# Loading v of two batch pairs through the SP queue in transfers of eight partitions

## The chip, the cores and the metric

The kernel runs on one core of one Trainium2 chip. The metric is the device time of one execution in microseconds (us). A profiled execution has a span some 1.7 us shorter than its time, and all readings "at 400.66 us" count from the start of the span.

## The reference

Attention with a decay over 8 batches and 8 heads (576 positions, head dimension 64), then a mixing of 64 Fourier modes by complex 512 x 512 weights, then a channel mix. Cut to what matters:

```python
scores = scale * q @ k.T + cumulated_log_decay      # causal, softmax, times v
x = attention.transpose(0, 2, 1, 3).reshape(8, 576, 512)
X = rfft(x, axis=1)[:, :64]
Y = einsum('bmd,mde->bme', X, w_r + 1j * w_i)        # 2 x 64 x 512 x 512 floats
u = x + irfft(Y)
out = u + relu(u @ w_ch)
```

The mode weights are read once, 134 MB in float32. They make the kernel bound by DMA.

## The kernel before

The program walks through 16 batch pairs of attention and, between their steps, multiplies the mode weights as they arrive. Nearly every load is issued by GpSimd in one fixed order; the transfers of weights, k and q also convert float32 to bfloat16 on the way. The v of a pair stays float32. It goes into one of three staging buffers (`STG = 3`); the first pair's v already comes by the SP queue.

```python
def pool_dma(dst, src):
    keep(nc.gpsimd.dma_start(dst, src))          # one order for all GpSimd loads
# ... cut ...
def emit_loads(pr):
    dc, bp, _ = steps[2 * pr]
    for nm, src in (("k", k), ("q", q), ("v", v)):
        one = src[2 * bp, 2 * dc, :, :]
        dst = QKVst[pr % STG][nm][:, :, :, :].rearrange("p b r d -> p b (r d)")
        ap = bass.AP(tensor=one.tensor, offset=one.offset,
                     ap=[[NR * Dh, 128], [H * S * Dh, 2], [1, NR * Dh]])
        if nm == "v" and pr < 1:
            nc.sync.dma_start(dst, ap)
        else:
            pool_dma(dst, ap)
# ... cut: in emit_transposes, the only reader of v ...
ins = nc.vector.tensor_tensor(sb, st, wdec9_of_this_pair, ALU.mult)
```

`NR * Dh` is 9 x 64 = 576 floats. So v of a pair is 128 partitions x 2 batches x 2,304 bytes, in all 576 KB.

The softmax here doesn't subtract the row's maximum and nothing guards it: scores larger than these inputs give would overflow.

## Time and profile before

| | before |
|---|---|
| time, median of 3 runs | 437.25 us (436.92 to 439.48) |
| profiled span | 437.0 us (that execution took 438.78 us) |
| last weight transfer has landed on all 16 DMA engines | 400.66 us |
| from there to the end | 36.3 us |
| landings of that transfer, first to last engine | 392.63 to 400.66 us |
| v of the 9th pair: issued, read | 88.11, 122.82 us |

The profile has a strip for DMA (one digit for each fortieth of the span, 9 is busy for 90% or more), a table of queues (packets, MB, the time of their packets as a share of sixteen engines' span), and a chain of waits (start, length, what). The trace has two finer records: a semaphore increment for each engine that finishes its share of a transfer, and the start and length of each DMA packet. Neither names an engine. The increments of a transfer therefore tell how far apart the engines are. "Offset" below is an engine's increment minus that of the foremost engine for the same transfer.

### The profile page before, as it was taken

Reading aid. Unit: us, or ns where it says so; the run is one execution under the profiler, and the core shown is the slowest. Engines: PE = TensorE matmul, PEld = TensorE weight load, DVE = VectorE, ACT = ScalarE, POOL = GpSimd, SP = SyncE. Lnnn points to the kernel's source line nnn. Section 1 sums busy time; section 2 is a strip of 40 time slices with the busy share of each in tenths; the row PEclk is TensorE's granted clock in tenths of the full one; section 3 lists DMA queues with packets and bytes.
Section 4 is the critical chain, followed back from the end, with each engine's and each line's share of the span. In section 5 each row is a group of like instructions: output and inputs, shape, how many; then the busy total and the mean of one; then the engine's idle time right before and its main releaser. Section 6 shows DMA issues by size and latency. Waiting matters only on the chain.

```text
span 437.0 us, 12197 instructions
## 1 busy us (share of the span) xinstructions
PE 359.5 (82%) x5247; PEld 245.5 (56%) x5265; DVE 263.3 (60%) x658; ACT 224.6 (51%) x340; POOL 128.9 (29%) x202
## 2 busy tenths in 40 slices
PE   3787799998897887978778796999999688998880
PEld 2454666676666665656556664666665354554440
DVE  5797778877565655655657677333334353753891
ACT  2887478775534537446355473234335242742780
POOL 7333332233233233232332231323232223200600
PEclk9996699998866858556668688699999898998997
DMA  8999999999999999999999999999999999993797
GB/s 185 233 235 244 230 236 238 237 214 234 233 215 236 228 220 237 211 237 233 215 237 211 211 212 211 211 211 211 211 211 212 211 211 211 211 207 73 253 366 270
DMA packets 50981, 97.37 MB, mean 223 GB/s; under 512 B 3792, under 2 KB 12976, under 8 KB 50928
## 3 DMA queue, kind: packets, MB, share of 16 engines
q0 software_dynamic: 46688, 86.16, 100.6%
q1 hardware_dynamic: 3920, 9.91, 6.3%
q8 instruction: 41, 0.67, 0.6%
q10 hardware_dynamic: 320, 0.52, 0.5%
q14 instruction: 12, 0.10, 0.1%
HBM read 163.73 MB, written 9.44 MB: 396 GB/s over the span
## 4 chain that ended last, share of the span: by engine, by line
PE 31%; DMA 29%; ACT 12%; DVE 11%; issue 4%; ACTq 0%; DVEq 0%; POOL 0%
DMA wb<-in_moe_w_i_dram 27%; ACT E L574 8%; PE pav L612 7%; PE ps L567 6%; PE A L188 5%; PE tp L305 5%; DMA stv<-in_v_dram 3%; DVE QTs L320 2%; PE px L655 2%; PE vp L539 2%; ACT KT L318 2%; PE pz L826 2%; PE pu L826 1%; DVE os L1004 1%; DVE XT L669 1%
## 5 line engine op out<-in xcount | busy, mean ns | idle before, releaser
L574 ACT ACTIVATE E<-ps 128x1024 bf16<-128x1024 f32 (+1 forms) x128 | 101.5, 853 | 22.8 <-PE ps L567 12.7
L188 PE MATMUL A<-XT,wb 128*128 128x16 bf16 x1984 | 70.3, 181 | 14.6 <-DMA wb<-in_moe_w_i_dram 9.6
L188 PEld LDWEIGHTS <-wb 128*128 128x128 bf16 x1984 | 63.5, 99 | 28.6 <-issue 11.9
L93 POOL DMA_DIRECT2D wb<-in_moe_w_r_dram x64 | 42.5, 664 | 120.7 <-DMA wb<-in_moe_w_r_dram 24.5
L567 PE MATMUL ps<-QTs,KT 64*128 64x64 bf16 (+4 forms) x384 | 57.6, 320 | 18.2 <-ACT E L574 16.3
L93 POOL DMA_DIRECT2D wb<-in_moe_w_i_dram x64 | 42.4, 663 | 86.6 <-DMA wb<-in_moe_w_i_dram 42.9
L612 PE MATMUL pav<-va,E 128*128 128x65 bf16 (+1 forms) x1088 | 55.5, 210 | 3.1 <-DVE x_all L634 2.6
L612 PEld LDWEIGHTS <-E 128*128 128x128 bf16 (+1 forms) x1088 | 45.5, 115 | 17.5 <-issue 8.1
L589 DVE TENSOR_TENSOR E<-E,trimask 128x256 bf16<-128x256 bf16 (+2 forms) x128 | 36.9, 303 | 20.2 <-ACT E L574 20.0
L324 ACT COPY VT<-tp 128x640 bf16<-128x640 bf16 (+1 forms) x32 | 23.2, 762 | 33.5 <-PE tp L305 33.5
L865 ACT CAST XW<-pxw 128x512 bf16<-128x512 f32 x36 | 20.7, 586 | 35.8 <-PE pxw L858 23.5
L567 PEld LDWEIGHTS <-KT 64*128 64x128 bf16 x384 | 19.2, 99 | 32.8 <-issue 21.1
L908 ACT CAST XW<-pB 128x512 bf16<-128x512 f32 x36 | 20.9, 586 | 31.4 <-PE pB L826 25.8
L318 ACT COPY KT<-tp 128x640 bf16<-128x640 bf16 (+1 forms) x32 | 22.0, 751 | 26.2 <-PE tp L305 26.0
L907 DVE CAST x_all<-pA 128x512 bf16<-128x512 f32 x36 | 24.9, 692 | 16.7 <-PE pA L826 15.2
L858 PE MATMUL pxw<-wch,yy 128*128 128x512 bf16 x133 | 33.7, 386 | 1.2 <-issue 0.7
L320 DVE COPY QTs<-tp 128x640 bf16<-128x640 bf16 (+1 forms) x32 | 23.3, 767 | 14.2 <-PE tp L305 14.0
L634 DVE TENSOR_TENSOR x_all<-pav,rcp 128x384 bf16<-128x384 f32 x64 | 29.2, 456 | 0.9
L153 DVE TENSOR_TENSOR YTe<-A,Yacc 128x128 bf16<-128x128 f32 x16 | 5.9, 368 | 33.2 <-PE A L188 33.2
L623 DVE RECIPROCAL rcp<-pav 128x6 f32<-128x6 f32 x64 | 12.1, 190 | 22.6 <-PE pav L612 21.8
L826 PEld LDWEIGHTS <-ident_bf 64*64 64x64 bf16 (+1 forms) x300 | 14.5, 110 | 17.0 <-issue 9.6
L539 PE MATMUL vp<-ident_bf,VT 128*128 128x128 bf16 x160 | 17.2, 249 | 4.8 <-DVE QTs L320 4.3
(143 smaller groups left out, 609.8 us busy)
## 6 DMA issues: line engine op xcount, KB each, us to landing
wb<-in_moe_w_r_dram POOLq DMA_DIRECT2D x62, 512.0 KB, 17.2
wb<-in_moe_w_i_dram POOLq DMA_DIRECT2D x62, 512.0 KB, 17.8
stv<-in_v_dram POOLq DMA_DIRECT2D x10, 576.0 KB, 15.4
out_dram<-os SPq DMA_DIRECT2D x10, 512.0 KB, 6.3
stk<-in_k_dram POOLq DMA_DIRECT2D x11, 288.0 KB, 15.4
stq<-in_q_dram POOLq DMA_DIRECT2D x11, 288.0 KB, 15.2
wx<-in_v_dram POOLq DMA_DIRECT2D x5, 576.0 KB, 15.1
out_dram<-uo SPq DMA_DIRECT2D x3, 512.0 KB, 3.6
```

Of the source, the lines that this page charges most:

```text
L93: keep(nc.gpsimd.dma_start(dst, src))
L188: nc.tensor.matmul(A[:, eb, mi, :], lhsT=w_of(mi, eb * 128), rhs=x_of(m), start=(i == 0), stop=(i == len(terms) - 1),)
L318: nc.scalar.copy(rows(KTs[pr % 2][:, :, 0:S]), tv)
L320: ins = nc.vector.tensor_copy(rows(QT[pr][:, :, :]), tv)
L539: nc.tensor.transpose(vp[:, sc, :, :].rearrange("p b d -> p (b d)"), VTs[s // 2 % 2][:, h, sc * 128 : (sc + 1) * 128], ident_bf[:, :],)
L567: nc.tensor.matmul(ps[:, b, o : o + n], lhsT=KTs[pr % 2][bs, h, jb * 128 : (jb + 1) * 128], rhs=QT[pr][bs, h, jb * 128 + c0 : jb * 128 + c ...
L574: nc.scalar.activation(E[:, :, piece * 512 : piece * 512 + w], ps[:, :, 0:w], ACT.Exp, scale=scale,)
L589: nc.vector.tensor_tensor(dg, dg, tr, ALU.mult)
L612: nc.tensor.matmul(pav[64 * half : 64 * half + w, slot, :], lhsT=E[:, b, c : c + (w - 1) * st + 1 : st], rhs=va[:, jb, b, :], start=(n == ...
L634: nc.vector.tensor_tensor(xo, pi, ri, ALU.mult)
L826: return nc.tensor.matmul(p, lhsT=lhsT, rhs=rhs, start=first, stop=not first, skip_group_check=True)
L858: nc.tensor.matmul(pxw[:, :], lhsT=xT[:, eb, i * 128 : (i + 1) * 128], rhs=wch[:, eb, :], start=(eb == 0), stop=(eb == NDC - 1),)
```

## The change

It takes v of the ninth and thirteenth pair off the GpSimd queue. Sixteen SP transfers of eight partitions take its place, presumably meant to run on eight of the sixteen DMA engines only, so that the other eight are relieved.

```diff
+    EIGHTS = (8, 12,)
...
                 if nm == "v" and pr < 1:
                     nc.sync.dma_start(dst, ap)
+                elif nm == "v" and pr in EIGHTS:
+                    for p in range(0, 128, 8):
+                        nc.sync.dma_start(
+                            dst[p : p + 8, :, :],
+                            bass.AP(
+                                tensor=one.tensor,
+                                offset=one.offset + p * NR * Dh,
+                                ap=[[NR * Dh, 8], [H * S * Dh, 2], [1, NR * Dh]],
+                            ),
+                        )
                 else:
                     pool_dma(dst, ap)
```

## The prediction

> **What bounds the kernel now.** I read the page first: the DMA strip, the queue table and the chain of work that ended last. The DMA engines are busy at 0.9 or more from the second slice until the weights have landed, the GpSimd (software) queue alone fills 100.6% of sixteen engines' span, and the largest piece of the chain is the landing of weights:
>
> ```profile
> DMA  8999999999999999999999999999999999993797
> q0 software_dynamic: 46688, 86.16, 100.6%
> q1 hardware_dynamic: 3920, 9.91, 6.3%
> q8 instruction: 41, 0.67, 0.6%
> ```
>
> Then the chain in order of time for 270 to 396 us. From 276 us on it is one weight load after another, and TensorE starts the tile before last 0.05 us after the last of them:
>
> ```profile
> 276.12 18.28 DMA wb<-in_moe_w_i_dram
> 294.40 0.29 issue
> 294.69 19.60 DMA wb<-in_moe_w_i_dram
> ...
> 375.30 19.72 DMA wb<-in_moe_w_i_dram
> 395.02 0.05 issue
> 395.07 0.91 PE A L188 x30
> ```
>
> So anything on DMA that delays the last weight delays the end one to one, and anything that only makes one stage of attention quicker is worth nothing. The tail behind the last landing (400.66 us, below) is 36.3 us of TensorE, VectorE and output and is not touched.
>
> The wait list says how GpSimd meets this: it waits for the transfer issued eight earlier, over and over. Eight software transfers are in flight, and a transfer counts as landed only when its slowest engine has finished.
>
> ```profile
> POOL wb L93 <- DMA wb<-in_moe_w_r_dram: 55.2, 31, 2.5
> POOL wb L93 <- DMA wb<-in_moe_w_i_dram: 55.2, 33, 2.7
> ```
>
> **The sixteen engines are not equally late.** The trace records each of the sixteen completion increments of every transfer. I grouped them by semaphore, sixteen to a transfer, and looked at the spread from first to last. It is 1.1 us for the first weight transfer, 2.5 us near 60 us, 3.6 us near 140, 5.1 us near 220, 6.2 us near 290 and 8.03 us at the very last weight transfer, whose increments fall from 392.63 to 400.66 us. The foremost engine is never idle: it takes 2.47 us for each weight transfer all the way through. At the last transfer the offsets from the foremost engine are 0, 0.01, 0.13, 0.19, 0.52, 0.73, 1.69, 3.29, and then 4.82, 4.93, 6.50, 6.80, 6.85, 6.97, 7.14, 8.03: eight early engines and eight late ones. The late ones move back in single steps of 1.1 to 1.5 us, and the steps fall at the times of the 41 packets of the instruction queue (16,384 bytes, median 959 ns each; their lengths repeat with a period of eight, 974, 974, 961, 893, 893, 949, 945, 936 ns). So TensorE's instruction blocks are fetched by eight engines in turn, and those eight end the weights 3 to 8 us after the others. The early engine at 3.29 moved in smaller steps, of about 0.5 us, beside the 8,192-byte instruction packets of the other engines. I take this change to be aimed at that imbalance.
>
> **What the Trainium skill says.** In "DMA: Bandwidth & Descriptors", the section on why a DMA increments its semaphore by 16 says that a DMA runs on the largest k up to 16 that divides the slowest dimension of both sides, and that from SP these are the lowest-numbered k engines. Eight partitions then mean engines 0 to 7, one partition each. The trace before has no transfer that shows it. The same page, "Queues, rings and completion order", says that an engine takes its queue rows in turn, packet by packet; the SP load of the first pair's v, 4.3 us from issue to landing against a median of 15.4 us for the GpSimd ones, agrees, though little was queued then. "Runtime: NRT & Kernel Launch", "Instruction fetch mechanics", gives 16 KiB instruction blocks; 0.67 MB in 41 packets is 16.3 KB each, which agrees. No page that I found says which engines fetch TensorE's instructions, and the trace has no engine numbers. That is the open point.
>
> **The change part by part.** Removed: two of the GpSimd transfers of v, 576 KB each. An engine's share is 8 packets of 4,608 bytes at 178 ns, 1.42 us; the completion records give 1.47 us from q's landing to v's on one engine. All sixteen engines lose 2 x 1.47 = 2.94 us. GpSimd also loses two issues of 0.73 us, which fill none of its waits.
>
> Added: 32 SP transfers of 8 x 2 x 576 floats (36 KB each). If they run on the eight lowest engines, each engine moves 16 x 2 = 32 packets of 2,304 bytes per pair. At the 93 ns that such packets took for the first pair this is 2.98 us, with 16 completion writes of 22 ns 3.33 us; at the rate of the present weights (4,096 bytes read per packet, 16 packets in 2.47 us, 26.5 bytes per ns) it would be 2.78 us. So those eight gain 5.6 to 6.7 us for the two pairs and lose 2.94: 2.6 to 3.7 us net each.
>
> Moved: the two v transfers now wait on SP for the staging buffer only (multiplies of v at 75.34 and 142.07 us), not in GpSimd's order (issues at 88.11 and 158.44). They land earlier, and their users come late anyway: the multiplies of those pairs start at 122.82 and 195.66 us, while v has landed at about 101.8 and 174.7. The emitted order confirms it: SP gains twice sixteen loads, GpSimd loses two, and TensorE and VectorE only shift a few instructions.
>
> Sum, if engines 0 to 7 are the early ones: the late eight end at 8.03 - 2.94 = 5.1, the early ones at most at 3.29 + 2.6 to 3.7 = 5.9 to 7.0. The last landing moves from 8.03 to 5.9 to 7.0, a gain of 1.0 to 2.1 us: 437.25 becomes 435.2 to 436.2. The eight early engines, not the late ones, then bound the end; that is why the whole 2.9 us can't be had.
>
> **Rivals.** (a) Engines 0 to 7 are the fetching, late ones, or the fetching ones are spread over both halves. Then the latest engine gains 2.6 to 3.7 us of work and the end moves to 439.9 to 440.9 us. Nothing in the trace rules it out. Against it speaks the shape of the change: sixteen small transfers instead of one are an odd price to pay unless the other eight engines needed relief, and two pairs take 2.9 us off an imbalance whose group means differ by about 5.7 us, about half of it, which is what levelling wants. I give the favourable case 75%.
>
> (b) The wait for v on the chain goes away. The chain has
>
> ```profile
> 88.11 11.64 DMA stv<-in_v_dram
> 99.75 0.01 issue
> 99.77 0.42 DVE Yacc L197
> 100.19 1.26 DVE vb L291
> ```
>
> which looks like 11.64 us to win, some 2.7%. But the timeline names the operand of that multiply:
>
> ```profile
> 100.10 1.35 DVE L291 TENSOR_TENSOR vb<-wx,wdec 128x1152 bf16<-128x1152 f32 x1
> ```
>
> It reads wx, another pair's v, which landed at 85.09 us; the transfer issued at 88.11 is read at 122.82, 21 us after it lands. The chain put the wait down to the semaphore's latest update. Were (b) true the time would be near 426; I give it 1%.
>
> (c) The SP issues become a wait: each transfer from the ninth on waits for the one eight before it. Sixteen issues at 0.56 us and two rounds of landings take perhaps 10 to 15 us, against 46 and 52 us from free buffer to use. It is hidden: no effect. Nor does SP have other work before 389 us.
>
> (d) Many small descriptors slow the weights on the same engines by more than their own length. This would push the early engines past 8 us and give 437.5 to 439.
>
> **Range and chances.** Weighted: 75% for 435.2 to 436.2 with some leak towards 437.5, the rest near 440.5. The weight of the favourable case puts my figure at 435.9; 434.6 to 440.6 holds both outcomes. Two per cent is 8.7 us, more than any of the sums, so within 2% is nearly certain. A slow run of the kernel before was at 439.48, so single runs will not settle this.
>
> **What would show it.** Right: in the changed kernel the last weight lands 1 to 2 us earlier than 400.66; the spread of its completion increments shrinks to 6 or 7 us; the two SP loads each put a step of 1.3 to 1.9 us on eight early engines, while the late ones draw nearer; 256 packets of v per pair on the hardware queue. Wrong: the spread grows to 10 or 11 us, with the steps on the engines that were late already (rival a); a foremost engine that idles; waits of VectorE for v; or a last landing that moves while the end does not, because the tail is bound by TensorE.

## More of the kernel before

Repeated executions of one kernel mostly agree within 0.3%, though on one of the chips used here the kernel before ranged from 436.5 to 440.7 us. Differences of under one per cent are therefore read from when work ends in the trace as well as from the times.

## The result, and the profile after

| | before, same chip | after |
|---|---|---|
| time, median | 437.7 us (436.92 to 439.48, 4 runs) | 443.22 us (441.71 to 444.41, 4 runs) |
| profiled span | 437.0 us | 441.1 us |
| last weight landed | 400.66 us | 405.46 us |
| from there to the end | 36.3 us | 35.6 us |
| landings of the last weight, first to last | 392.63 to 400.66 us | 393.06 to 405.46 us |

The ratio is 1.0119, with a 95% interval from 1.0073 to 1.0164. The change made the kernel slower by 1.2%. The prediction was 435.9 us, a gain, and its range ended at 440.6.

The page of the changed kernel, DMA strip, rate for each fortieth of the span (11.0 us), and queue table:

```profile
DMA  8999999999999999999999999999999999993697
GB/s 182 233 235 246 228 235 238 230 210 211 225 222 237 229 227 210 210 235 225 224 233 215 211 212 211 211 211 211 212 211 212 210 211 211 211 199 64 232 366 283
q0 software_dynamic: 46400, 84.98, 99.4%
q1 hardware_dynamic: 4688, 11.10, 7.3%
q8 instruction: 41, 0.67, 0.6%
```

The strip is as full as before: busy time does not show the damage, since a slow packet counts as busy. (The rate of the eighth slice, 77 to 88 us, 230 GB/s while the first v was loaded, is compared further down with that of a kernel with the same bytes in the same place.) In the table 288 packets left q0 and 768 came to q1 for the same 1.2 MB. q1's share rose from 6.3% of 437.0 us to 7.3% of 441.1 us: times sixteen engines, from about 440 us to 515 us of engine time. That is 75 us (the rounding of the shares leaves some 7 us of doubt), or 9.4 us for each of eight engines, where the prediction had put 5.6 to 6.7.

The end of the chain of waits of the changed kernel (start, length, what):

```profile
369.75 19.60 DMA wb<-in_moe_w_i_dram
389.35 0.28 issue
389.63 15.82 DMA wb<-in_moe_w_i_dram
405.46 0.05 issue
405.50 0.36 PE A L173 x8
```

Weight load follows weight load as before, and the last is 4.8 us later. One thing is different. In the chain of the kernel before, which the prediction shows to 395.07 us, the last wait for DMA ends at 395.02; from there on TensorE and VectorE are at work, and the last weight, landed at 400.66 us, is used only at 401.25, some 0.5 us later:

```profile
400.40 0.29 PE A L172 x8
400.69 0.33 PE pu L826 x2
...
401.25 0.29 PE A L172 x8
```

In the changed kernel TensorE waits for the last weight and starts 0.05 us after it. This slack is most of why the span grew by 0.7 us less than the landing moved.

No wait of VectorE for v came up. The last packets of the two SP loads start at 92.5 and 161.7 us, and the multiplies that read them at 122.83 and 195.68 us. The list of instructions that touch v (count, duration min/median/max in ns, first and last start in us):

```profile
L277 SPq DMA_DIRECT2D stv<-in_v_dram x32: 272/273/544, 76.4 to 155.7; - x32
L302 DVE TENSOR_TENSOR vb<-stv,wdec x11: 1348/1352/1359, 15.3 to 254.4; 128x1152 bf16<-128x1152 f32 x11
```

The packet records tell where the extra engine time lies. These are the 256 packets of 2,304 bytes and 128 completion writes of each SP load (tabulated from the trace of the changed kernel):

```
                 data packet mean / median     completion mean
9th pair             150.5 / 134 ns                72.9 ns
13th pair            117.6 / 106 ns                20.1 ns
```

The prediction had assumed 93 and 22 ns. The v packets of GpSimd's queue that ran beside them (4,608 bytes) had medians of 254 to 266 ns, against 178 in the kernel before.

The offsets of the last weight transfer were 0, 0.37, 3.86, 3.95, 4.05, 4.07, 4.40, 4.74, and then 6.91, 7.00, 7.25, 7.70, 8.25, 10.44, 11.39, 12.40. I followed each offset through the transfers. The latest eight are the engines that carried the SP loads; they land 7.35 us later than the same engines before, on the mean (with the identification of the eight given under "map" below). The other eight end at 397.8 us, which is the old latest landing less the 2.9 us that had been predicted as their relief. Not all of them kept it: the two foremost engines landed at 393.06 and 393.43 us, no earlier than the foremost ones before (392.63). Two of the eight SP engines (11.39 and 12.40) still take steps of about 1.1 us from instruction fetches after 200 us.

### The profile page after: what moved, and what is told of

Same layout as the page of the kernel before. It is cut to its first block, busy times and chain, and to the rows that moved or that the text cites. A ratio compares the mean times of both kernels' runs of the same rounds, so it can differ in the third digit from the quotient of the medians.

```text
span 441.1 us, 12253 instructions
## 1 busy us (share of the span) xinstructions
PE 365.1 (83%) x5247; PEld 247.6 (56%) x5265; DVE 263.5 (60%) x658; ACT 225.9 (51%) x340; POOL 127.9 (29%) x200
## 4 chain that ended last, share of the span: by engine, by line
DMA 39%; PE 29%; ACT 9%; DVE 7%; issue 4%; DVEq 0%; ACTq 0%; POOL 0%
DMA wb<-in_moe_w_i_dram 39%; PE pav L623 6%; ACT E L585 6%; PE ps L578 6%; PE A L189 5%; PE tp L316 4%; PE pz L837 2%; DVE QTs L331 2%; PE vp L550 2%; PE pu L837 2%; PE px L666 1%; ACT VT L335 1%; ACT KT L329 1%; DVE vb L302 1%; PE px L691 1%
## 5 line engine op out<-in xcount | busy, mean ns | idle before, releaser
L578 PE MATMUL ps<-QTs,KT 64*128 64x64 bf16 (+4 forms) x384 | 59.3, 326 | 16.0 <-ACT E L585 13.8
L623 PE MATMUL pav<-va,E 128*128 128x65 bf16 (+1 forms) x1088 | 58.3, 215 | 3.6 <-DVE x_all L645 3.2
L623 PEld LDWEIGHTS <-E 128*128 128x128 bf16 (+1 forms) x1088 | 47.6, 118 | 17.5 <-issue 6.0
```

The lines of the kernel that those rows point to most:

```text
L578: nc.tensor.matmul(ps[:, b, o : o + n], lhsT=KTs[pr % 2][bs, h, jb * 128 : (jb + 1) * 128], rhs=QT[pr][bs, h, jb * 128 + c0 : jb * 128 + c ...
L623: nc.tensor.matmul(pav[64 * half : 64 * half + w, slot, :], lhsT=E[:, b, c : c + (w - 1) * st + 1 : st], rhs=va[:, jb, b, :], start=(n == ...
```

## The experiments

Unless said otherwise results are correct. The kernel before had a median of 437.17 to 437.19 us beside the first eight kernels and 437.47 beside the last four.

The explanations, by the numbers that some expectations use: **1**, each transfer costs each of its engines a fixed time; **2**, the confinement to eight engines slows these; **3**, each packet of the hardware queue costs some 0.16 us beside software packets; **4**, where in SBUF the eight partitions lie slows the packets (shared write ports); **5**, the DRAM side does (the eight engines read neighbouring rows). Besides these there is the question of membership: are the eight engines of the SP loads the early ones?

| kernel | each v load | packets, 9th / 13th pair, mean ns | last weight landed, us | ratio to before (95%) |
|---|---|---|---|---|
| before, two traces | one GpSimd transfer | - | 400.66, 400.29 | 1 |
| changed kernel | 16 x 8 neighbours | 150.5 / 117.6 | 405.46 | 1.0119 (1.0073 to 1.0164) |
| one16 | one SP transfer of 128 | 104 to 105.5 | 400.21 | 1.0013 (0.9998 to 1.0028) |
| p16 | 8 x 16 neighbours | 138 / 161 | 403.00 | 1.0069 (1.0049 to 1.0089) |
| b1 | 32 x 8 neighbours, one batch each | 106.9 / 106.4 | 402.51 | 1.0066 (1.0049 to 1.0083) |
| ports | 16 x 8, every fourth partition | 104.8 / 104.0 | 402.63 | 1.0085 (1.0056 to 1.0113) |
| rowsonly | neighbours in SBUF, rows four apart | 132.5 / 111.6 | 404.16 | single look |
| portsonly | every fourth in SBUF, neighbouring rows | 103.4 / 103.6 | 402.45 | single look |
| step2 | 16 x 8, every second partition | 106.4 / 104.5 | 402.71 | single look |
| ports1 | as ports, 9th pair only | - | 400.95 | 1.0046 (1.0023 to 1.0069) |
| nov | both v loads left out | - | 397.27 | 0.9947 (0.9913 to 0.9982) |
| low4 | 9th pair, half on four engines | 106.8 | 399.53 | 0.9979 (0.9948 to 1.001) |

**one16.** Both v loads go to SP, each as one transfer of 128 partitions.

```diff
+                elif nm == "v" and pr in EIGHTS:
+                    nc.sync.dma_start(dst, ap)
```

> The two v loads on the SP queue as one transfer of 128 partitions each, so on all sixteen engines: the queue changes, the confinement to eight engines and the small transfers do not come along. In the changed kernel the eight SP engines gained about 10.3 us of work gross for the two pairs, 5.15 per pair, or 0.161 us per packet of 2,304 bytes. Theory 1 (each small transfer costs its engines about 0.13 us beyond its packets): 16 packets of 0.093 and one completion, 1.6 us per pair against 1.47 before, so the end within 0.5 us of the kernel before. Theory 2 (eight engines are slowed because the load is confined to them): no confinement, so within 0.5 us. Theory 3 (a packet of the hardware queue itself costs 0.16 us beside software packets): 2.6 us per pair against 1.47, so all engines and the end come 2.2 us later.

437.68 us, 1.0013 of before, and the last weight at 400.21 us. The SP queue by itself, over all sixteen engines, costs nothing that can be seen. Explanation 3, which wanted 2.2 us more here, falls. So the loss comes from how the load is cut up and where it runs.

**p16.** Eight transfers of sixteen neighbouring partitions, which use all engines (cut: the access pattern has 16 rows too).

```diff
-                    for p in range(0, 128, 8):
-                            dst[p : p + 8, :, :],
+                    for p in range(0, 128, 16):
+                            dst[p : p + 16, :, :],
```

> Eight SP transfers of sixteen partitions per pair: each transfer still gives an engine two packets and one completion, as in the changed kernel, but all sixteen engines share them. Theory 1 (per transfer) and theory 3 (per packet): 8 x 0.32 = 2.6 us per engine and pair against 1.47, so all sixteen engines are later by 1.1 us per pair and the end by 2.2 us against before. Theory 2 (confinement): about as before, within 0.5 us.

440.12 us, and the last weight at 403.00. Even spread over all sixteen engines, the load is dear, so the confinement (2) is not needed for it: data packets of 138 and 161 ns and completions of 31 and 50 ns give 16 x 150 + 8 x 40 ns = 2.7 us per engine and pair. The foremost engine's own landing, 395.29 against 392.63, gives 2.8 per pair when the 1.47 that it saved is added back. With the 106 ns that other cuts show it would be 1.9 us. The page of p16 and the page of one16 show the difference in engine time at nearly the same bytes, first p16:

```profile
q1 hardware_dynamic: 4688, 11.10, 7.5%
```

and one16:

```profile
q1 hardware_dynamic: 4464, 11.09, 7.1%
```

**b1.** Twice as many transfers, with one packet for each engine in each.

```diff
                     for p in range(0, 128, 8):
+                        for b in range(2):
-                            dst[p : p + 8, :, :],
+                            dst[p : p + 8, b, :],
```

> Thirty-two SP transfers of eight partitions and one batch per pair: on the same eight engines the same packets and bytes as in the changed kernel, but twice the transfers and completions. Theory 1 (0.13 us per transfer): 16 more transfers are 2 us more per pair on those engines, so the last landing some 4 us later than in the changed kernel, near 447 us. Theories 2 and 3 (confinement, or per packet): the same as the changed kernel, 442 to 444 us.

440.04 us, last weight at 402.51: 32 transfers per pair were cheaper than 16. Explanation 1 falls; the 442 to 444 us of 2 and 3 did not come either. Data packets were back at 106.9 and 106.4 ns on the same neighbouring partitions. The gross cost per SP engine and pair works out as 32 x 106.7 + 32 x 21 ns = 4.1 us. So neighbouring partitions alone don't make packets slow; it also matters how they follow one another.

**map.** A diagnostic. The v of four pairs is cut so that SP transfers have 2, 4, 8 and 12 partitions, the rest of each v by GpSimd or the same queue, so that the sets of engines nest.

```diff
+    PLAN = {
+        5: ((2, 16, "sp"), (96, 1, "pool")),
+        8: ((4, 16, "sp"), (64, 1, "pool")),
+        11: ((8, 16, "sp"),),
+        14: ((12, 10, "sp"), (8, 1, "sp")),
+    }
```

> A look, not a candidate: v of pair 5 partly on two engines (16 transfers of 2 partitions), of pair 8 partly on four (16 of 4), of pair 11 wholly on eight (16 of 8), of pair 14 on twelve (10 of 12). If a transfer of n partitions runs on the n lowest-numbered engines, the completion records fall into nested groups of 2, 2, 4, 4 and 4 engines that are later by steps, and the steps of TensorE's instruction fetches later on show to which groups the fetching engines belong. My first reading (the eight fetching engines are the upper eight) wants no such step in the first eight; the trace of the changed kernel suggests that two of the first eight fetch and two of the upper eight do not. Time several us above the changed kernel, since two engines get some 15 us more.

Last weight at 406.20 us, time 444.38 us (one look). It told three things. First, with two partitions the record can be read packet by packet: a hardware-queue packet of 106 ns, then one software packet, and so on in turn, with a completion write of 22 ns. Two data packets and a completion take 0.234 us of an engine, sixteen such transfers 3.75 us. "Queues, rings and completion order" of the skill's "DMA: Bandwidth & Descriptors" has an engine take its rows in turn by packet; the trace agrees. Second, the data packets averaged 108 ns with two partitions, 106.5 with four, 129 with eight, 190 with twelve. Third, the nesting sorts the engines by how much each was pushed back. Among the most delayed, the offsets 10.01, 11.22 and 11.95 show no late fetch steps, while 9.97 and 10.09 do. This fits engines 0 to 3 without fetches, two fetching engines among 4 to 7, two among 8 to 11 and four among 12 to 15. So the eight engines of a transfer of eight partitions are six early ones and two fetching ones. That set is consistent with the changed kernel, where exactly two of the latest eight keep fetching; low4 tests it below.

The lengths of the instruction fetches, which repeat with a period of eight, say which two they are. Only two of the eight take 893 ns. In the kernel before, the engines that end at offsets 4.82 and 4.93 make their last steps (3.43 to 4.50 and 3.35 to 4.43) beside the fetches of 893 ns at 314.8 and 323.9 us. In the changed kernel the two loaded engines step (10.78 to 11.88 and 10.32 to 11.41) beside the fetches of 893 ns at 319.1 and 328.4 us. So the fetching engines under the SP loads are the ones that stood at 4.82 and 4.93.

**ports.** Eight partitions four apart in each transfer; both sides of the copy keep their meaning.

```diff
-                    for p in range(0, 128, 8):
-                            dst[p : p + 8, :, :],
+                    for n in range(16):
+                        p = 32 * (n // 4) + n % 4
+                            dst[p : p + 29 : 4, :, :],
-                                ap=[[NR * Dh, 8], ...
+                                ap=[[4 * NR * Dh, 8], ...
```

> The changed kernel, but each transfer takes every fourth partition (p, p+4, ... p+28) instead of eight neighbours; result correct. In the record of two engines alone (16 transfers of 2 partitions) a software packet stands between every two hardware ones and a transfer costs an engine 2 x 0.106 + 0.022 = 0.234 us, 3.75 us per pair, not the 5.15 that the changed kernel shows; there the hardware packets grow to 118 to 150 ns on average, software packets of v from 178 to 254 and more. Theory 4 (eight neighbouring partitions are two SBUF ports by the port map of the Trainium skill, four engines on each; every fourth partition is eight ports): packets back at 106 ns, 3.75 us per pair, net 2.28; the latest fetching engine of the first eight, 4.93 us before, ends at about 9.5 to 10 us, so the last weight 1.5 to 2 us after that of the kernel before, the time near 439. Theory 1 (a cost per transfer as such): 443 as the changed kernel.

Packets of 104.8 and 104.0 ns and completions of 19 ns: the slow packets are gone, and the GpSimd packets of v beside them are back at about 180 ns. The last weight landed at 402.63 us, 2.0 to 2.3 us after before, and 2.8 us earlier than in the changed kernel. The remaining loss is the two fetching engines among the eight (offsets 11.91 and 11.32): they land 5.1 and 4.6 us later than the two fetching engines of the set did before.

The skill's "SBUF — State Buffer", "Door 1: The DMA port swizzle", says that four neighbouring partitions share one of sixteen DMA ports, and that the next four lie on another. Then eight neighbours reach two ports, and eight partitions four apart reach eight. That is what suggested this run, and the runs agree with it as far as the next ones show.

**rowsonly and portsonly.** Ports changed both sides of the copy at once. These two, with wrong results, change one side each: rowsonly reads DRAM rows four apart into neighbouring partitions (the destination of the changed kernel), portsonly reads neighbouring rows into every fourth partition.

```diff
 rowsonly:  dst[8 * n : 8 * n + 8, :, :]   rows p, p+4, ... p+28
 portsonly: dst[p : p + 29 : 4, :, :]      rows 8n, 8n+1, ... 8n+7
```

> Wrong result on purpose: as ports on the DRAM side (rows 4 apart), but into eight neighbouring partitions as in the changed kernel. Theory 4 (SBUF ports): slow packets and a last weight near 405 us as in the changed kernel. Theory 5 (engines that read neighbouring DRAM rows hinder each other): packets of 106 ns and a last weight near 402.5.

> Wrong result on purpose: neighbouring DRAM rows as in the changed kernel, but into every fourth partition. Theory 4 (SBUF ports): packets of 106 ns, last weight near 402.5. Theory 5 (DRAM rows): slow packets, last weight near 405.

The packets stayed slow in rowsonly (132.5 and 111.6 ns, last weight 404.16) and were fast in portsonly (103.4 and 103.6 ns, last weight 402.45). So it is the placement in SBUF, not the rows in DRAM: 5 falls, and of explanation 4 the placement is shown, the shared ports are not (see step2). Rowsonly's packets were a little shorter than the changed kernel's, but the same cut had 129 ns in map, so this lies within its own spread. The page of portsonly, to be held against that of the changed kernel at equal packets and bytes, shows it without packet records:

```profile
GB/s 179 234 235 240 235 235 238 250 220 211 233 215 236 234 237 210 210 237 230 218 236 213 211 212 211 211 211 211 211 211 211 211 211 211 211 202 78 230 364 298
...
q1 hardware_dynamic: 4688, 11.10, 7.0%
```

The eighth number is 250 instead of 230. 7.0% of 437.5 us times sixteen is 490 us, 25 us less than in the changed kernel, or 1.6 us for each of eight engines and pair.

**step2.** Eight partitions two apart, two engines to a port by the skill's map.

```diff
+                        p = 16 * (n // 2) + n % 2
+                            dst[p : p + 15 : 2, :, :],
```

> Correct, both pairs: sixteen transfers of eight partitions two apart, so that two instead of four of the eight engines write through one port of SBUF. Theory of shared ports: packets of 2,304 bytes take between those of the changed kernel (150.5 and 117.6 ns on average) and those of every fourth partition (104.8 and 104.0), nearer the latter, near 106 ns, and the last weight lands 402.5 to 403.5. If only transfers with neighbouring partitions in a run are slow, also 104 to 106. If it is something else in the pattern of the changed kernel that any eight partitions close together bring, 118 to 150 and a last landing near 405.

Packets of 106.4 and 104.5 ns, last weight 402.71 us: held, two engines on a port are not slow. But sharing of ports as such isn't the whole story. In map, four engines on one port were at 106.5 ns, and in b1 the eight neighbours were fast with one packet each. In these runs the slowing came only with transfers of eight to sixteen neighbouring partitions that put two packets on each engine. What exactly collides stays open.

**ports1.** As ports, for the ninth pair only, on the idea that half the load would leave the SP engines below the others.

> Every fourth partition, and only the ninth pair. Eight engines gain 3.75 - 1.47 = 2.28 us, the others lose 1.47. From the offsets of the kernel before: the latest fetching engine of the first eight 4.93 + 2.28 = 7.2, of the others 8.03 - 1.47 = 6.6, so the last weight 0.8 us earlier than before and the time 0.8 us less, if the loads' cost is what theory 4 says. At the changed kernel's 3.7 us net it would be 8.6, 0.6 us later than before.

438.66 us, ratio 1.0046: a loss where a gain had been expected. The two fetching SP engines came last (offsets 9.65 and 9.06). They landed 2.9 and 3.4 us later than before, where 3.75 - 1.47 = 2.3 had been worked out; so 0.6 to 1.1 us of it is not accounted for. Even at 2.3 us, the later of the two would have landed at 397.56 + 2.3 = 399.8 us, only 0.8 earlier than the end before. A load on this set of eight lands on two engines that have only some 3 us of room (8.03 less 4.93).

**before2, nov, low4** ran together on another chip.

> The kernel before, unchanged, profiled on another chip run, so that the readings by step and engine do not rest on one trace alone. Every theory: last weight landing 400.7 us to within 0.5, increments 8.0 us apart to within 0.3, two lanes near 4.8 to 5.0 between the eight early and the six late ones, the instruction fetch packets of 893 to 974 ns in a rotation of eight.

The kernel before again: 400.29 us instead of 400.66, spread 7.43 instead of 8.03 us, same two lanes at 4.97 and 5.02. The spread missed its expectation by 0.3 us, so a difference of half a microsecond in one trace's last landing means nothing here. In this trace the last weight is on the chain: TensorE starts 0.05 us after it, at 400.34 us. It also gave a warning on the chain. This is its summary for before2, where the page before has DMA at 29%, with the same program:

```profile
DMA 39%; PE 27%; ACT 10%; DVE 7%; issue 4%; DVEq 0%; ACTq 0%; POOL 0%
```

and this the one of the changed kernel:

```profile
DMA 39%; PE 29%; ACT 9%; DVE 7%; issue 4%; DVEq 0%; ACTq 0%; POOL 0%
```

The share of DMA in the chain depends on where the walk back changes from DMA to an engine that ended nearly as late. That it is higher after the change says nothing on the change.

> Wrong result on purpose: the v loads of the ninth and thirteenth pair are left out altogether, on every queue. This measures what the removed half of the change is worth by itself. The account by engine says that all sixteen engines lose 2 x 1.47 = 2.94 us, so the last weight lands 2.9 us earlier than in the kernel before (near 397.7) and the kernel takes 434.3 us; the spread of the last transfer's increments stays at 8.0 us. The rival, that the two loads filled gaps or that the end is bound elsewhere, gives less than 1.5 us. With this as the base, the added half in the changed kernel is the last landing of the changed kernel minus this one.

```diff
+                elif nm == "v" and pr in EIGHTS:
+                    pass
```

Without the two loads (wrong result) the last weight landed at 397.27 us, 3.0 to 3.4 earlier, and the time was 435.68 us, ratio 0.9947. In landing the removed half of the change is worth the predicted 2.9 us; in time it was 1.8 us by the medians (0.8 to 3.8 by the interval), less than the 2.9 us expected here too. The added half moves the landing by 405.46 - 397.27 = 8.2 us. The spread did not stay at 8 but shrank to 5.4 us: the foremost engine landed only 0.7 us earlier, and so did not use its room (at 284.9 us its next landing came 4.39 us after the one before, where 2.47 is the rule). That part of the expectation missed; the latest engine sets the last landing.

> Correct, ninth pair only. Half of v (64 partitions) by sixteen SP transfers of four partitions four apart, which the account puts on engines 0 to 3 alone, the engines that fetch no instructions; the other half by one GpSimd transfer of 64 partitions over all sixteen. Engines 0 to 3 take 16 x 4 half-size packets more: gross 3.75, less the 0.73 of the half that left the GpSimd queue and less 0.73 more of... net 3.75 - 0.73 = 3.0 us, from at most 3.3 (perhaps 4.9 for one) to at most 6.3 (7.9) behind the foremost; the other twelve lose 0.73 us. So the last weight lands 0.7 us earlier than in the kernel before and the kernel takes 436.5 us (ratio 0.998). If one of engines 0 to 3 is a fetching one after all, the last weight lands 2 to 3 us later (ratio 1.005 to 1.007). If a transfer costs the same whatever its placement, the same as the first.

```diff
+    EIGHTS = (8,)
+                    for n in range(16):
+                        p = 16 * (n // 4) + n % 4
+                        nc.sync.dma_start(dst[p : p + 13 : 4, :, :], ...)   # 4 partitions
+                    pool_dma(dst[64:128, :, :], ...)                        # the other half
```

Correct, and the only cut that gained: last weight at 399.53 us, 0.8 to 1.1 earlier than before. Four offsets took steps of about 2 to 3 us while the load ran, and the largest offset was 7.13. The time, 437.01 us with a ratio of 0.9979 (0.9948 to 1.001), is where it was expected but can't be told from none. Had one of the four engines been among the six latest, the end would have moved back by 1.5 to 3 us. This supports engines 0 to 3 as the ones without fetches. The packets, four to four ports, were at 106.8 ns.

## Why the prediction was wrong

**What held.** DMA bounds the kernel, and a later last weight means a later end: +4.8 us in landing, +4.1 us in the profiled span, +5.5 us in the medians. "One to one" is too strong: in the kernel before, the last landing had some 0.5 us of slack, and from it to the end the fourteen traces have 34.9 to 37.0 us. The relief was 2.9 us for the latest engine without the load in the changed kernel and 3.0 to 3.4 in nov. The SP loads run on eight engines: the sixteen increments of each come as one immediate update and eight landings, as the skill's section quoted in the prediction has it. The first SP transfer was issued at 76.41 us and all of v of the ninth pair had landed by about 93, so rival (c), a wait on SP, stayed hidden. Rival (b), a wait for v that goes away, did not come.

**First failing step, the size.** "each engine moves 16 x 2 = 32 packets of 2,304 bytes per pair. At the 93 ns ... with 16 completion writes of 22 ns 3.33 us". It measured (7.35 + 2.94) / 2 = 5.15 us. The terms: 32 packets at 106 ns, the length that well placed packets have amid weight traffic in every run, make 3.39, and 16 completions of 22 ns make 0.35, together 3.74 us. The 93 ns of the first pair's v, at a time with little else queued, did not carry over. The rest is placement. Packets were longer than 106 ns by 44.5 in the ninth and 11.6 in the thirteenth pair, times 32 on the mean 0.90 us; completions of 72.9 and 20.1 instead of 22 ns add 0.39 on the mean. The sum is 5.03 of the 5.15. Portsonly and rowsonly show that the destination partitions make this part; by what mechanism stays open. The trace before has no SP packets of this size amid weight traffic, so it could have shown neither 106 nor 150.

**Second failing step, the membership.** "If engines 0 to 7 are the early ones". Six of them are; two fetch instructions and stood at 4.82 and 4.93 before, where the prediction allowed 3.29 at most. The arithmetic of the prediction itself, with 4.93 and the predicted 2.6 to 3.7, gives 7.5 to 8.6 against 8.03: from a small gain to a small loss. With the measured 7.35 it gives 12.3; the two engines measured 11.82 and 12.83, counted like these from 392.63 us. So membership alone would have taken away the gain, and size alone, from 3.29, would have given 10.6, a loss of 2.6 us. Both were needed for 4.8.

**The weight of rival (a).** It said fetching engines among those loaded, 439.9 to 440.9 us, with a spread of 10 or 11. The kernel without slow packets (ports) came to 440.92 us and a spread of 11.9. Rival (a) was the right one in kind, and was given a quarter because sixteen small transfers looked like something done for a reason. The form of a change is no evidence of where its author's premise is right. The figure of 435.9 was that of the favourable case; weighted with the chances given, 75% of 435.7 and 25% of 440.4, it would have been 436.9. Rival (d), small descriptors that slow others, was right in kind too, by GpSimd's v packets at 254 to 266 instead of 178 ns, but its 439 us stops short since it assumed a slowing without the wrong engines.

**Left open.** What makes neighbours slow with eight to sixteen partitions to a transfer but not with four, or with one packet each; the 0.6 to 1.1 us of ports1; and which two of engines 4 to 7 fetch.

## What to carry to other kernels

When DMA is full, work out what each engine carries, not the mean: transfers on fewer than sixteen engines help only if none of those engines is among the latest, and the last transfer's sixteen completion increments show how far apart the engines are, though not which is which; a test transfer of a few partitions tells that. When a load is cut into transfers of eight or so partitions, try every second or fourth one instead of neighbours: here this brought the packets from 118 to 150 ns back to 103 to 106. Where this load left the software queue as one transfer of 128 partitions, no cost could be seen (1.0013); cut into sixteen transfers of eight neighbours it cost 1.2%.

## What the Trainium skill lacked or had wrong

- "Runtime: NRT & Kernel Launch", "Instruction fetch mechanics", gives the block size but not which DMA engines fetch, nor the cost to them: here eight engines in turn, 893 to 974 ns a packet and 1.1 to 1.5 us of delay each, 41 times, which left the last weight's landings 8.0 us apart. Two of these engines are among the eight lowest, none among the four lowest as far as map and low4 tell.
- "DMA: Bandwidth & Descriptors" says on how many engines a transfer runs, but not that packets grow longer when each transfer goes to a few neighbouring partitions: 118 to 150 ns per packet of 2,304 bytes with eight, 138 to 161 with sixteen, 190 with twelve, against 103 to 105 with eight partitions four apart.
- "SBUF — State Buffer", "Door 1: The DMA port swizzle", gives the map of ports that led to the cure and the bandwidth of one port, but not when sharing a port makes packets longer: two engines on a port (106.4 and 104.5 ns) and four on a single port (106.5 ns) showed no cost, four on each of two ports did (150.5 and 117.6 ns) unless each transfer had one packet per engine (106.9 and 106.4 ns).
